# Threshold attention with a feed-forward block: raw weight chunks in the rooms of the turned blocks and exponentials, and chunk work at other places of slots six to ten

## The chip, the cores and the metric

The kernel runs on one core of one Trainium2 chip. The metric is the device time of one execution in microseconds (us); lower is better. Times that are compared are medians of several executions; a profile is one execution, with its own time.

## The reference, cut to what matters

```python
# q, k, v: (8 batches, 8 heads, 576, 64) float32; tau = 0.02
scores = 1/8 * q @ k^T
scores = where(scores >= rowmax(scores) - tau, scores, -1e9)
attn   = exp(scores - rowmax) ; attn /= rowsum(attn) + 1e-9
x      = (attn @ v) with the heads side by side        # (8, 576, 512)
xn     = (x - mean) / sqrt(var + 1e-6) * g_ln
out    = x + relu(xn @ w_ch1) @ w_ch2                  # 512 -> 2048 -> 512
```

Both weight matrices arrive as **float64**. The kernel has to turn them into float32 itself, from the two 32-bit words of each number.

## The kernel before, in words

**Slots.** The attention is cut into 72 slots (`NS`, 9 for each batch), one pass of the loop `for n in range(NS)` (L1072) each. Attention slots are numbered from 0. In a slot, TensorE (PE) makes the scores of four 128 x 576 blocks (L400), VectorE (DVE) takes their maxima (L414), GpSimd (POOL) makes thresholds (L418), ScalarE (ACT) the exponentials (L427), DVE masks and sums them (L434, reciprocals L439), and POOL divides (L450). The exponentials lie in one of two rooms `e_room`: they alternate up to slot 6, and from slot 7 on only `e_room[0]` is used. From slot 6 (`FIRST`) on the blocks are then turned: DVE transposes them in 32 x 32 pieces into `et` (L524, `turn_blocks`), SyncE's queue (SP) sends `et` to a DRAM scratch `scr` (L531, L535) and, in the next slot, fetches `em` and `er` from there (L545 to L554, `fetch`), and PE multiplies them with the values (L593 in the next slot, L603 ahead of the scores of the slot after). Below, turn(7), scr(7), em(7) are those of slot 7. Before slot 6 PE turns the blocks itself (`tp`, `tr`).

**Feed-forward.** A group `g` is half a batch: 288 tokens. `first_part` computes relu(xn @ w_ch1) for 16 column blocks d (PE tile `p`, relu on ACT L791), `second_plain` (only for g = 0) the second product, four blocks m of 16 matmul steps each, whose results ACT copies (L829) and DVE and POOL finish (L705, L706, L711, `add_to_x`, `store`); later groups use `second_quarters`. These steps are drawn in by `second_part(n, i)` (L997) at four places i = 0 to 3 of a slot, so many as a planner's count `owed` says. The PE order of attention and feed-forward is thus fixed when the program is made. All these products share two PSUM banks (tag `ff`): a product waits until ACT has read out the one before the last.

**Weight chunks.** The float64 weights come in 32 chunks of 512 KB (`Weights`): 0 to 15 make up w_ch1, 16 to 31 w_ch2. Each goes through five steps:

- `fetch` (L245): a DMA on SP's queue into a free piece of some room (`piece` takes, of the free pieces that may hold this chunk, the one whose time ends first). Rooms: parts of `w2_sb` that are not written yet, of `hidden`, of an `x` and a `y` tile, and of `stage`. In the profile the rooms have the names `w`, `hidden`, `x_room`, `y_room`, `stage` and `e`.
- `prepare_to` (L267): ACT takes the absolute value of the upper words (L273, "abs") and, at this or a later call, scales the lower words (L278, "low").
- `begin` (L282): three DVE instructions, L288, L291, L295.
- `carry` (L300): a POOL addition (L303), for w_ch1 also a multiplication by g_ln (L306). It gives the piece back, so that a later fetch can use it.
- `begin_to` and `carry_all` run several of these. The table `BEGUN` (L1052) says for each slot up to which chunk `begin` has gone at three places of the slot: `masks_at` (between the maxima and the masks), `behind_at` (behind the masks), `end_at` (at the end of the slot).

`first_part` and `second_plain` don't issue a step whose chunk has not been carried in the order of the program (L779, L820), and on the chip the step waits for that carry's semaphore.

**Order of the queues.** Each engine takes its instructions in the order in which this loop issues them. So a relu that is issued behind three abs waits for them, and SP's next DMA waits until the one ahead of it is issued. `run_all(aside)` issues what `add_to_x`, `store` and `root` (the Newton step on DVE, L732 to L736) left over.

Of the kernel before, what the change touches and what calls it, by code (L numbers as in the profile page):

```python
# [8 lines left out]
F32 = mybir.dt.float32  # L9
# [9 lines left out]
def kernel(  # L19
# [40 lines left out]
    NB = S // 32  # L60
    TOK = S // 2
    QH = 256
    SLOTS = 2 * HP + 1
# [7 lines left out]
    att = ctx.enter_context(tc.tile_pool(name="att", bufs=2))  # L71
# [19 lines left out]
    e_room = [consts.tile([128, 4, S], F32, name=f"e{i}") for i in range(2)]  # L91
# [4 lines left out]
    def product(out, lhsT, rhs, **flags):  # L96


        for h in range(2):
            r = slice(64 * h, 64 * h + 64)  # L100
            nc.tensor.matmul(out[r], lhsT=lhsT[:, r], rhs=rhs, **flags)  # L101
# [75 lines left out]
    class Weights:  # L177
# [13 lines left out]
        def __init__(self):  # L191
            self.chunks = [
                (w1_sb[i][:, c : c + WC], w_ch1[i * 128 : (i + 1) * 128, c : c + WC], i)
                for c in range(0, DF, WC)
                for i in range(NK)
            ] + [
                (
                    w2_sb[:, m, d : d + 4].rearrange("p d c -> p (d c)"),
                    w_ch2[d * 128 : (d + 4) * 128, m * 128 : (m + 1) * 128].rearrange(
                        "(d p) c -> p d c", p=128  # L200
                    ),
                    None,
                )
                for m in range(NK)
                for d in range(0, ND, 4)
            ]
            self.n1 = NK * (DF // WC)
            self.fetched = self.prepared = self.converted = self.begun = self.carried = 0
            self.raw, self.ticks = {}, 2
            flat = lambda t: t.rearrange("p a b -> p (a b)")  # L210

            x_room = ffn.tile([128, NK, TOK], F32, tag="x", bufs=3, name="x_room")
            y_room = ffn.tile([128, NK, TOK], F32, tag="sq", bufs=1, name="y_room")
            stage = self.stage = consts.tile([128, 8, WC], F32, name="stage")

            n1 = self.n1
            self.free = []  # L220
            for t, n, before in (
                (w2_sb.rearrange("p m d c -> p (m d) c"), ND // 2, lambda p: n1 + 2 * p - 6),
                (hidden, 4, lambda p: 10),
                (x_room, 1, lambda p: 2 * n1),
                (y_room, 1, lambda p: 2 * n1),
                (stage, 4, lambda p: 2 * n1),
            ):
                for p in range(n):
                    self.free.append((before(p), -1, flat(t)[:, p * 2 * WC : (p + 1) * 2 * WC]))
# [94 lines left out]
    FIRST = HP + 2  # L324

    def by_blocks(n):

        return n >= FIRST
# [346 lines left out]
    aside, stores, drops = [], [], []  # L675
# [22 lines left out]
    def run_all(calls):  # L698
        now = calls[:]
        calls.clear()  # L700
        for fn in now:
            fn()
# [294 lines left out]
    def second_part(n, i):  # L997

        nonlocal issued, owed, part, now
        part, now = i, QUARTERS * n + i  # L1000
        if not queue:
            return
        at = QUARTERS * n + i
        g = sum(issued >= e for e in ends)
        left = sum(ROOM[t % QUARTERS] for t in range(at, ready(g + 1))) if g + 1 < NG else 0
        owed += (ends[g] - issued) * ROOM[i] / left if left > 0 else 8


        steps = 0
        got = 1 if i in (0, QUARTERS - 1) else 2  # L1010
        while queue and (owed >= 0.5 or got == 1 and i in (0, QUARTERS - 1)):
            got, cost = next(queue[0], (None, 0))
            if got is None:
                queue.pop(0)
                got = 1
            elif got == 0:
                owed = 0.0
                break
            else:
                issued += cost  # L1020
                owed -= cost
                steps += 1
                if steps == 4 and among:
                    mean_of(among[0])
                    centre(among.pop())
# [11 lines left out]
    conversion = Weights()  # L1037
    if w_ch1.dtype == I64:
        conversion.fetch(2)
    else:  # L1040
# [10 lines left out]

    BEGUN = [  # L1052
        (0, 0, 1), (2, 2, 3), (4, 4, 5), (6, 6, 7), (8, 8, 9), (10, 10, 11),
        (13, 16, 17), (19, 22, 22), (25, 27, 27), (29, 31, 31), (32, 32, 32),
    ]

    def constants(times):

        warm = ps_ff.tile([128, QH], F32, tag="ff", name="warm")
        for _ in range(times):  # L1060
            product(warm[:, :128], lhsT=avg_sb, rhs=ident, start=True, stop=True)

    def convert(to):
        conversion.begin_to(to)
        conversion.carry_all()
# [6 lines left out]
    for n in range(NS):  # L1072
        b, s = divmod(n, SLOTS)
        masks_at, behind_at, end_at = BEGUN[min(n, len(BEGUN) - 1)]
        run(n, -3)
        if 0 < n <= HP:
            constants(8 if n > 1 else 26)
        scores(b, s)
        run(n, -2)
        run(n, -1)  # L1080
        if n == FIRST + 1:
            conversion.take(e_room[1])
        if n + 1 < HP:
            scale_q(n + 1, loaded[n + 1][0])
        rest = exponentials(n)
        es, thr = next(rest)
        run(n, 0)
        if n == HP + 2:
            next(rest, None)
        if n >= HP:  # L1090
            conversion.fetch(3, -1 if n > FIRST else 1)
        run_first(stores)
        if n == FIRST:
            convert(masks_at)
        elif n > FIRST + 1:
            conversion.prepare_to(masks_at, False)
        second_part(n, 0)
        while drops and drops[0][0] is nc.gpsimd:
            drops.pop(0)[-1]()
        next(rest, None)  # L1100

        u = (n + 1) // SLOTS * HP + (n + 1) % SLOTS
        if (n + 1) % SLOTS < HP and u < len(units):
            turn(u)
            if u + 1 < len(units) and u != 2:
                load_qk(u + 1 if u > 1 else 3)
        if n < HP:
            conversion.fetch(2 if n else 1)
        if n < SLOTS + HP:
            run_all(aside)  # L1110
        if n != FIRST:
            convert(masks_at)
        conversion.prepare_to(*((end_at,) if n < FIRST else (behind_at, False)))
        run(n, 1)
        second_part(n, 1)
        blocks_go = by_blocks(n)
        diags = weights(es, thr, blocks_go)
        run_all(aside)
        drip()
        if n < SLOTS:  # L1120
            run_all(stores)
        conversion.begin_to(behind_at)
        run(n, 2)
        second_part(n, 2)
        if n < FIRST:
            conversion.carry_all()
        box = []
        if blocks_go:
            conversion.fetch(3, wait=0)
            scr = turn_blocks(b, s, es)  # L1130
            conversion.carry_all()
            at_quarter(n + 1, 0, lambda b=b, s=s, scr=scr, box=box: box.append(fetch(b, s, scr)))
        else:

            made = turn_weights(s, es, diags)
            for i, at in enumerate(
                (-1, -1, 0, 0)
            ):
                if i == 3 and n + 1 == FIRST:
                    at_quarter(n + 1, 0, conversion.prepare_to, BEGUN[n + 1][0], False)  # L1140
                if i < 3:
                    at_quarter(n + 1, at, next, made)
                else:
                    at_quarter(n + 1, at, lambda made=made, box=box: box.append(next(made)))
        at_quarter(
            n + 1, 1 if b == 0 and s <= HP else 3,
            lambda b=b, s=s, box=box: values_of(b, s, box[0]),
        )
        if s in (HP, 2 * HP):
            group_ready(2 * b + (s > HP))  # L1150
        run_all(aside)
        drip({nc.vector: 4, nc.gpsimd: 6})
        if HP <= n < FIRST:
            conversion.fetch(3)
        run(n, 3)
        if b == 0 and s < HP - 1:
            load_v(s + 1)
        elif n >= SLOTS - 2 and (n + 2) % SLOTS < HP and n < NS - 2:
            load_v((n + 2) // SLOTS * HP + (n + 2) % SLOTS)
        if n <= FIRST:  # L1160
            conversion.prepare_to(BEGUN[n + 1][0] - (n == FIRST - 1), n < FIRST)
        second_part(n, 3)
        conversion.begin_to(end_at)
        conversion.carry_all()
        run_all(aside)
        drip({nc.vector: 2, nc.gpsimd: 0})
    while later_calls or queue or aside or stores or drops:
        n += 1
# [38 lines left out]
```

## Time and profile before

| what | value |
|---|---|
| median of 3 runs | 1350.99 us (1350.66 to 1351.26) |
| the profiled execution's own time | 1349.67 us |
| its span, first to last instruction | 1347.7 us (1.97 us lie around it) |
| mean granted TensorE clock | 0.997 |
| PE busy in 80 to 100, 100 to 120, 120 to 140 us | 19.75, 18.15, 17.69 of 20 us |
| PE busy in 140 to 160, 160 to 180 us | 15.71, 17.46 of 20 us |
| PE busy in 180 to 1260 us | 1075.35 of 1080 us |

The scores of slots 6, 7, 8, 9, 10 and 11 start at 70.8, 98.0, 116.4, 137.2, 162.7 and 182.8 us of the span. So the chunks' work, which ends in slot 10, lies in the first 172 us, and the other seven eighths of the span have PE busy throughout. In a timeline line the columns are: start and duration in us, engine (with a q: its queue issues a DMA), line, operation, tiles out<-in, shape, number of instructions merged, and in brackets the idle time before and what ended it.

### The profile page before, as it was taken

How to read it: one execution, taken by the hardware profiler on the slowest of the kernel's cores; microseconds unless marked ns; L12 is line 12 of the kernel's file. 1: busy time of each engine (PE TensorE's matmuls, PEld its weight loads, DVE VectorE, ACT ScalarE, POOL GpSimd, SP SyncE). 2: the span in 40 equal slices, each digit the busy share in tenths (PEclk: the TensorE clock that was granted, in tenths of full speed). 3: DMA queues.
4: the chain of work that ended last, by engine and by line, in shares of the span. 5: the costliest groups of instructions: out<-in, count | busy, mean ns of one | idle time of the engine just before them, and what ended most of it. 6: DMA issues, size and time to landing. Idle time of an engine off the chain costs nothing.

```text
span 1347.7 us, 40452 instructions
## 1 busy us (share of the span) xinstructions
PE 1316.4 (98%) x17400; PEld 995.8 (74%) x17400; DVE 872.4 (65%) x1544; ACT 459.2 (34%) x995; POOL 624.7 (46%) x836
## 2 busy tenths in 40 slices
PE   8998899999999999999999999999999999999997
PEld 7765557769686786968778696877869677786957
DVE  7889876667666675666756677556756667666113
ACT  5866333232423233232233324233232323333120
POOL 3475656535444444444534454443444445335312
PEclk9999899999999999999999999999999999999999
DMA  8918864467643775446644576447754376443211
GB/s 166 304 32 248 205 178 156 158 172 193 178 150 118 197 196 162 151 156 190 178 145 153 162 179 192 141 142 194 198 169 152 123 198 179 134 159 124 81 19 20
DMA packets 335299, 213.94 MB, mean 159 GB/s; under 512 B 247376, under 2 KB 292688, under 8 KB 327056
## 3 DMA queue, kind: packets, MB, share of 16 engines
q1 hardware_dynamic: 329008, 210.46, 54.2%
q8 instruction: 137, 2.24, 0.7%
q10 hardware_dynamic: 5952, 0.74, 0.4%
q0 software_dynamic: 160, 0.15, 0.1%
q14 instruction: 42, 0.34, 0.1%
HBM read 124.00 MB, written 87.29 MB: 157 GB/s over the span
## 4 chain that ended last, share of the span: by engine, by line
PE 91%; DVE 3%; ACT 3%; SPq 1%; DMA 1%; issue 1%; POOL 1%; ACTq 0%; POOLq 0%; DVEq 0%
PE p L101 37%; PE seg L101 30%; PE sc L400 10%; PE sc L593 9%; PE sc L603 2%; ACT e L427 1%; PE tp L101 1%; DVE e L434 1%; SPq L118 1%; PE var L101 1%; DVE neg L414 1%; PE mean L101 0%; ACT em L484 0%; PE pv L593 0%; PE warm L101 0%
## 5 line engine op out<-in xcount | busy, mean ns | idle before, releaser
L101 PE MATMUL p<-xc,w 128*64 128x288 f32 x4096 | 517.0, 408 | 5.5 <-ACT part L878 4.9
L101 PEld LDWEIGHTS p<-xc,w 128*64 128x64 f32 x4096 | 287.9, 137 | 212.2 <-issue 14.3
L414 DVE TENSOR_REDUCE neg<-sc 128x2 f32<-128x1152 f32 x144 | 188.7, 1352 | 286.4 <-PE sc L400 286.1
L450 POOL TENSOR_SCALAR e<-e,den 128x576 f32<-128x576 f32 x264 | 207.4, 798 | 130.0 <-DVE den L439 130.0
L101 PE MATMUL seg<-hidden,w 128*64 128x144 f32 x3840 | 247.9, 287 | 0.0
L101 PEld LDWEIGHTS seg<-hidden,w 128*64 128x64 f32 x3840 | 234.9, 137 | 11.5 <-issue 8.6
L434 DVE SCALAR_TENSOR_TENSOR e<-sc,thr,e 128x576 f32<-128x576 f32 x288 | 222.3, 809 | 18.9 <-POOL thr L418 11.7
L418 POOL TENSOR_SCALAR thr<-neg,low_sb 128x2 f32<-128x2 f32 x144 | 39.8, 277 | 383.5 <-DVE neg L414 382.1
L791 ACT ACTIVATE hidden<-p 128x288 f32<-128x288 f32 x256 | 106.5, 417 | 300.8 <-PE p L101 300.8
L427 ACT ACTIVATE e<-sc,neg 128x576 f32<-128x576 f32 x288 | 198.1, 754 | 2.4 <-DVE neg L414 2.4
L524 DVE STREAM_TRANSPOSE et<-e 128x1152 f32<-128x1152 f32 x118 | 161.2, 1373 | 14.3 <-POOL e L450 13.7
L400 PE MATMUL sc<-kT,qT 64*64 64x384 f32 (+3 forms) x2048 | 138.6, 403 | 1.3 <-DVE e L434 1.2
L593 PE MATMUL sc<-em,v_in 128*64 128x128 f32 (+1 forms) x2368 | 131.2, 265 | 2.6 <-DMA em<-scr 2.6
L593 PEld LDWEIGHTS sc<-em,v_in 128*64 128x64 f32 x2368 | 124.2, 138 | 10.9 <-DVE w L288 2.4
L101 PE MATMUL seg<-hidden,stage 128*64 128x144 f32 x1920 | 123.3, 286 | 0.0
L101 PEld LDWEIGHTS seg<-hidden,stage 128*64 128x64 f32 x1920 | 117.6, 137 | 2.9 <-issue 2.9
L616 ACT COPY x<-sc 128x128 f32<-128x128 f32 x120 | 31.8, 266 | 252.9 <-PE sc L400 182.1
L863 POOL TENSOR_TENSOR hidden<-hidden 128x576 f32<-128x576 f32 x60 | 84.7, 1427 | 51.9 <-ACT hidden L791 42.3
L400 PEld LDWEIGHTS sc<-kT,qT 64*64 64x64 f32 x2048 | 75.8, 133 | 41.7 <-issue 21.4
L878 ACT COPY part<-seg 128x288 f32<-128x288 f32 x74 | 29.8, 403 | 190.6 <-PE seg L101 187.1
L863 DVE TENSOR_TENSOR hidden<-hidden 128x576 f32<-128x576 f32 x60 | 51.1, 886 | 51.5 <-PE seg L101 48.5
L799 POOL TENSOR_TENSOR hidden<-hidden 128x288 f32<-128x288 f32 x48 | 39.5, 822 | 47.1 <-ACT hidden L797 44.6
(121 smaller groups left out, 1077.9 us busy)
## 6 DMA issues: line engine op xcount, KB each, us to landing
scr<-et SPq DMA_DIRECT2D x63, 1152.0 KB, 5.0
em<-scr SPq DMA_DIRECT2D x63, 1024.0 KB, 5.7
out_dram<-ot SPq DMA_DIRECT2D x248, 36.0 KB, 3.8
q_in<-in_q_dram SPq DMA_DIRECT2D x120, 72.0 KB, 2.6
er<-scr SPq DMA_DIRECT2D x132, 64.0 KB, 5.1
k_in<-in_k_dram SPq DMA_DIRECT2D x116, 72.0 KB, 2.8
v_in<-in_v_dram SPq DMA_DIRECT2D x28, 256.0 KB, 5.4
w<-in_moe_w_ch_dram SPq DMA_DIRECT2D x11, 512.0 KB, 6.4
```

The costliest lines, as they stand in the source:

```text
L101: nc.tensor.matmul(out[r], lhsT=lhsT[:, r], rhs=rhs, **flags)
L400: nc.tensor.matmul(sc[h][64 * i : 64 * i + 64, at : at + n], lhsT=ql[r] if s == HP else qT[r, half, j * 128 + 64 * i : j * 128 + 64 * i + 64],
L414: nc.vector.tensor_reduce(out=neg[:, i], in_=pairs[h], axis=AXL.X, op=ALU.max, negate=True,)
L418: nc.gpsimd.tensor_scalar(out=thr[:, i], in0=neg[:, i], scalar1=-1.0, scalar2=low_sb, op0=ALU.mult, op1=ALU.add,)
L427: nc.scalar.activation(es[:, i], blocks[i], func=AF.Exp, bias=neg[:, i : i + 1])
L434: nc.vector.scalar_tensor_tensor(out=es[:, i], in0=blocks[i], scalar=thr[:, i : i + 1], in1=es[:, i], op0=ALU.is_ge, op1=ALU.mult, accum_o ...
L450: nc.gpsimd.tensor_scalar(out=es[:, i], in0=es[:, i], scalar1=den[:, i : i + 1], scalar2=1.0, op0=ALU.mult, op1=ALU.mult,)
L524: nc.vector.transpose(et[:, :, 64 * h : 64 * h + 64].rearrange("p n (j c) -> p j n c", j=2), es[:, 2 * h : 2 * h + 2].rearrange("p j (n c) ...
L593: nc.tensor.matmul(dst[64 * h : 64 * h + 64], lhsT=vt[:, h, c, :], rhs=pick(em[:, 2 * j : 2 * j + 2, c], h), start=c == 0 and first, stop= ...
L791: nc.scalar.activation(hidden[:, d], p1, func=AF.Relu)
L799: nc.gpsimd.tensor_tensor(out=sq[:, 0], in0=sq[:, 0], in1=sq[:, c], op=ALU.add)
L863: eng.tensor_tensor(out=out[at], in0=in0[at], in1=in1[at], op=op)
```

## The change

It has four parts.

1. **Rooms.** The tile of the turned blocks, `et`, which is not used before slot 6, holds two raw chunks (below chunk 13). `e_room[1]` is lent for raw chunks right behind turn(6) instead of at the start of slot 7.
2. **Requests.** `fetch(5)` instead of `fetch(3)` at the end of slots 4 and 5; `fetch(2)` behind turn(6), into the room just lent. By the lists of free pieces, chunks 22 and 23 are now requested in slot 5 and 24 and 25 in slot 6 behind scr(6) (before: all four in slot 7); 26 to 28 in slot 7 (before: 25 to 27 with 22 to 24), 29 to 31 in slot 8 behind em(7) and er(7) (before: 28 to 30 there, and 31 ahead of scr(8)).
3. **Counts.** `BEGUN` runs ahead. Begun by slot, at the three places:

| slot | before | after |
|---|---|---|
| 6 | 13, 16, 17 | 13, 16, 19 |
| 7 | 19, 22, 22 | 21, 23, 24 |
| 8 | 25, 27, 27 | 26, 27, 29 |
| 9 | 29, 31, 31 | 31, 32, 32 |
| 10 | 32 | 32 |

4. **Places.** From slot 7 on the abs for the masks' chunks go behind the slot's last relus (end of the slot before) instead of ahead of the relus; those of `behind_at` go behind `second_part(n, 1)`; those of `end_at` (and, behind them, the lows) ahead of turn. In slots 6 to 10 the two late `run_all(aside)` are left out, so that the Newton step of g = 0 goes from the end of slot 7 to behind the maxima of slot 8, and the finishing of its four results (o, ot, store) goes to later places, the first store from slot 9 to slot 10.

```diff
+            et_room = att.tile([128, NB, 128], F32, tag="et", bufs=1, name="et_room")
...
+                (et_room, 2, lambda p: n1 - 3),
...
-        (13, 16, 17), (19, 22, 22), (25, 27, 27), (29, 31, 31), (32, 32, 32),
+        (13, 16, 19), (21, 23, 24), (26, 27, 29), (31, 32, 32), (32, 32, 32),
...
+    def plain_at(n):
+
+        return FIRST <= n <= SLOTS + 1
...
-        if n == FIRST + 1:
-            conversion.take(e_room[1])
...
-        elif n > FIRST + 1:
-            conversion.prepare_to(masks_at, False)
         second_part(n, 0)
...
-        conversion.prepare_to(*((end_at,) if n < FIRST else (behind_at, False)))
+        if n < FIRST:
+            conversion.prepare_to(end_at)
+        elif n == FIRST:
+            conversion.prepare_to(behind_at, False)
         run(n, 1)
         second_part(n, 1)
+        if n > FIRST:
+            conversion.prepare_to(behind_at, False)
...
             conversion.fetch(3, wait=0)
+            conversion.prepare_to(end_at, False)
             scr = turn_blocks(b, s, es)
+            if n == FIRST:
+                conversion.take(e_room[1])
+                conversion.fetch(2)
             conversion.carry_all()
...
-        run_all(aside)
+        if not plain_at(n):
+            run_all(aside)
...
-            conversion.fetch(3)
+            conversion.fetch(5)
...
-        if n <= FIRST:
-            conversion.prepare_to(BEGUN[n + 1][0] - (n == FIRST - 1), n < FIRST)
+        if n < FIRST:
+            conversion.prepare_to(BEGUN[n + 1][0] - (n == FIRST - 1))
         second_part(n, 3)
         conversion.begin_to(end_at)
         conversion.carry_all()
-        run_all(aside)
+        if FIRST <= n < SLOTS:
+            conversion.prepare_to(BEGUN[n + 1][0], False)
+        if not plain_at(n):
+            run_all(aside)
```

The order of PE's own instructions is the same before and after: the planner draws the same feed-forward steps at the same places of slots 6 to 11, since no step was kept back for a chunk in either order.

## The prediction

> **What bounds the kernel now.** I read the page, then busy time by stretch, then PE's timeline where PE is not full.
>
> ```profile
> span 1347.7 us, 40452 instructions
> ...
> PE   8998899999999999999999999999999999999997
> ```
> ```profile
> 140.00:160.00 20.00, 15.71 (x130) 10.07 (x128) 18.28 (x34) 7.71 (x14) 12.60 (x15) 0.86 0.82 198
> 160.00:180.00 20.00, 17.46 (x168) 10.26 (x166) 15.34 (x31) 6.49 (x13) 9.93 (x14) 0.97 0.74 185
> ```
>
> From 180 us on PE is the bound (1075.35 of 1080 us busy up to 1260): time saved before 180 us moves all that follows forward, and nothing can be saved behind it by this change. Before it PE waits in the chunk stage; the last numbers of a row are the granted clock (0.86 there), DMA share and GB/s. PE's timeline names the waits:
>
> ```profile
> 118.45 4.10 PE L101 MATMUL p<-xc,w 128*64 128x288 f32 x32
> 124.86 8.47 PE L101 MATMUL p<-hidden,w 128*64 128x288 f32 x68 [2.31 <-ACT hidden L791]
> 133.12 1.95 PE L593 MATMUL sc<-em,v_in 128*64 128x128 f32 x32
> 134.87 2.14 PE L101 MATMUL p<-hidden,w 128*64 128x288 f32 x16
> ...
> 152.28 1.19 PE L101 MATMUL p<-hidden,w 128*64 128x288 f32 x8 [1.65 <-POOL w L303]
> 153.92 0.44 PE L593 MATMUL sc<-em,v_in 128*64 128x128 f32 x4 [0.45 <-DMA em<-scr]
> 156.56 3.25 PE L593 MATMUL sc<-em,v_in 128*64 128x128 f32 x28 [2.19 <-DMA em<-scr]
> 159.57 2.95 PE L101 MATMUL p<-hidden,w 128*64 128x288 f32 x16
> ...
> 172.86 2.16 PE L101 MATMUL p<-hidden,w 128*64 128x288 f32 x16 [2.54 <-POOL w L303]
> ```
>
> To see: with a wait of 1.85 us at 106.07 (var, behind a relu) these are five places. At 122.55 and 106.07 a relu lies behind three abs on ACT; at 150.64 and 170.32 a product waits for the carry of chunk 27 and 31; in between PV of slot 8 waits for em(8). From 154.4 to 161.2 us the clock is at half: 28 products take 3.25 us where 32 take 1.95, and 16 take 2.95 where they took 2.14: 1.55 + 0.81 = 2.4 us lost. **Ceiling** of the change: 1.85 + 2.31 + 1.65 + 0.45 + 2.19 + 2.54 + 2.4 = 13.4 us.
>
> The chain that ended last runs from 132 to 151 us over SP's queue, whose timeline shows what makes em(8) late:
>
> ```profile
> 128.76 1.64 SPq L257 DMA_DIRECT2D stage<-in_moe_w_ch_dram  x3
> 130.50 7.19 SPq L118 DMA_DIRECT2D q_in<-in_q_dram  x4
> 137.73 2.67 SPq L118 DMA_DIRECT2D k_in<-in_k_dram  x4
> 140.50 0.91 SPq L257 DMA_DIRECT2D e<-in_moe_w_ch_dram  x1
> 141.51 4.20 SPq L531 DMA_DIRECT2D scr<-et  x4
> ```
>
> et(8) is turned at 140.11, but SP reaches scr(8) at 141.51, with three chunks of 512 KB and q and k ahead of it; four issues of q take 7.19 us, so the DMA engines are full. By the trace's landings k ends at 142.72, chunk 31 at 145.31, scr(8) at 149.68, em(8) at 156.42.
>
> **What the Trainium skill says.** (1) TensorE: Matmul & The Clock Gate, Part 1: the clock halves after an idle window of 3.4 us and returns after a busy one; windows run free. The trace agrees: one stretch at half clock, 6.83 us long, behind the waits around 150 to 156 us; the 2.54 us wait alone brought none. (2) The same page, Architectural detail: ACT and DVE queues are strictly first in, first out; the relus behind the abs agree. (3) SBUF — State Buffer, SBUF: two separate sides: DVE with two SBUF inputs or in a 2-port mode and POOL lock each other out. The trace agrees: begin's three instructions take 0.41, 0.43, 0.69 us at 102.7, and 0.82, 0.80, 1.66 us at 95.2, while POOL carries. (4) DMA: Bandwidth & Descriptors, Issuing engines are not separate DMA queues: all DMAs run on the same 16 engines, so a chunk ahead of scr costs it time; here k, chunk 31 and scr(8) do land one after the other (142.72, 145.31, then up to 149.68).
>
> **The change, part by part.**
>
> *Up to 92.6 us* only rooms and requests differ: chunks 17, 18, 22, 23 are asked for earlier on SP, in 50 to 65 us. Behind them SP has nothing until scr(6) at 95.3: nothing gained or lost.
>
> *Tail of slot 6* (95 to 103 us). Two begins and two carries more ahead of slot 7's maxima and thresholds. DVE before: begin 16 from 95.22 to 98.57, scores at 100.1, maxima at once. After: three begins, between 1.5 us each alone (end 99.9, no loss) and 3.35 each as that one (105.3). I take 2.4, as begins beside POOL's division take: 102.5. Maxima end at 103.9 and 105.2 (1.35 each; before 101.50 and 102.76). POOL: abs 16 to 18 now go ahead of low 13 to 15 on ACT, 3 x 0.58 = 1.75 us, so carry 15 starts at 96.2, not 94.44; three w_ch1 carries take 6.75 as before, to 102.95, three w_ch2 carries 3 x 1.29: 106.8; thresholds 107.4 (before 103.22).
>
> *PE in slot 7.* Two exponentials (1.38) from 103.9, relu of d = 8 to 105.7. PE ends d = 9 at 104.05 and needs that bank: waits 1.7, ends d = 10 at 107.8. Exponentials to 107.0, low 19 and 20 to 108.2, relu to 108.5, var; abs 21 and 22 still stand ahead of the next relu, to 110.1. The product behind var starts at 110.2, before at 108.45: **1.75 lost**, although the change put abs behind one relu.
>
> *turn(7).* Masks wait for thresholds and begins 19, 20: from 108.8 (before 105.72), 3.35 us. Carries 20, 19 to 111.5, division 3.95: 115.45; two begins under it instead of three, to 116.2; turn(7) ends at 118.9 (before 117.48): **+1.4**, from 0 (begins uncontended; POOL's 107.4 then decides) to 6.5 (all begins 3.35).
>
> *Slot 8.* Begin 23 (1.55) takes the place of the Newton step (2.43) ahead of the maxima: they start at 120.5 (before 119.82). No abs ahead of the relus: relu d = 14 at 124.0, PE ends d = 15 at 124.2 and starts `second_plain` at 124.3 (before 124.86): the 2.31 us are gone, 0.5 of it is left after slot 7's loss. em(7) lands 1.4 later, at 133.3: PE, there at 132.5, waits 0.8. So PE's own gain is spent here; it costs nothing, since the next wait swallows it.
>
> *SP in slots 6 and 7.* Chunks 24 and 25 now stand between scr(6) and em(6): 1.1 us of issue and about 3 us of DMA (chunks land 1.5 us apart). em(6) landed at 107.55, er(6) at 108.83; PV of slot 6 comes at 112.8, after at 114.3: hidden, with 2 us left. Fetch 26 waits for carry 18 (104), 27 and 28 for carries 20 and 19 (111.5); behind them stands scr(7), due only at 118.9: free.
>
> *em(8).* SP's slot 8 has the same three chunks at the same place and all of it 1.4 later; chunk 31 is gone from between k and scr(8): 145.31 - 142.72 = 2.6 us of DMA. em(8): 156.42 + 1.4 - 2.6 = 155.2 (bounds: +1.4 if the chunk's share was hidden anyway, -2.6 if turn(7) is on time). The gate of chunk 27 goes, as it is carried at the end of slot 8, but PE then stands at PV by 152 and waits to 155.2 instead: of 4.29 us of waits 3.2 stay. PV starts **1.25 earlier**. Clock: one idle stretch of 3.2 us instead of three pieces; I take the same 2.4 us lost (bounds: none, or 1.7 more for a further half window at half clock).
>
> *Slot 10.* Chunk 31 is carried in slot 9: **2.54 gained**. What is late next: the centring of g = 1 on DVE; maxima 2.6, turn 2.3, two leftovers 0.9 behind scores that end at 164.1 put it at 170.2 to 171.8, when PE is there too (171.8): I take 0.3 off. em(9) is fetched earlier, with the store of m = 0 gone from between; PV of slot 10 has 7 us of room. The stores moved to slots 10 to 12 lie under a full PE: nothing.
>
> **Sum:** -1.25 - 2.54 + 0.3 = -3.5 us: 1349.67 - 3.5 = 1346.2 us of this execution, which is 1.32 us below the median; against the median 1350.99 - 3.5 = **1347.5**.
>
> **Rivals.**
> - *All covers go.* If begins hide (turn(7) on time) and the DMA engines catch up by 4 us, PE doesn't wait for em(8), and the clock stays: 4.29 + 2.4 + 2.54 = 9.2: 1341.8. For it: in slot 7 three chunks are requested instead of six. Against: q, k and three chunks stay ahead of scr(8). Chance 0.15.
> - *Gain given back.* PV no earlier, the longer idle stretch costs another half window (1.7): -2.54 + 1.7 = -0.8: 1350.2. Chance 0.15.
> - *Slower.* Six carries ahead of slot 7's thresholds and three begins ahead of its maxima: one mechanism, on POOL and DVE, that goes through turn(7), scr(7), em(7) and SP to em(8). From turn(7) later by 2.6 + 2.54 = 5.1 us it ends slower. At 6.5, with the further half window: 6.5 - 2.6 - 2.54 + 1.7 = +3.1: 1354.1. For: DVE is 95% busy there. Against: only one begin before took 3.35. Chance 0.2.
> - *It doesn't do what it says* (a chunk is requested earlier but its carry still gates): the counts put carries 27 and 31 a slot's quarter or more ahead; below 0.05, within the second rival.
>
> **Numbers.** Forecast 0.5. What can be told from no change is about 0.2%, 2.7 us: faster means below 1348.3. Of the forecast's 0.5, 0.38 lie below that; with the first rival 0.53. Within: 0.12, the second rival 0.15, 0.05 of the third: 0.32. Slower: 0.15. The range, 1342 to 1353, leaves half of the first rival and most of the third out.
>
> **What would show it.** No wait ahead of `p<-hidden,w` near 123, 151 and 171 us; PE waits in slot 7 of 2.5 us or more ahead of d = 10, var and the next product; maxima of slot 7 at 102 to 103; turn(7) ended at 118 to 120; one wait of PV for em(8) of about 3 us, ended near 155; still one stretch at half clock. Wrong if turn(7) is past 122.6, or if em(8) lands by 152.

## The result and the profile after

| | before | after |
|---|---|---|
| median of 12 executions each | 1350.49 us | 1350.38 us |
| ratio of the times, with its 95% interval | | 1.0003 (0.9996 to 1.0011) |
| the profiled execution's own time | 1349.67 us | 1351.38 us |

The change makes no difference that can be measured. (The ratio is not that of the two medians; the means are 1350.19 and 1350.77 us.) The profiled execution of after lies 1.0 us above its median, that of before 0.8 us below: the two profiles differ by 1.7 us where the medians agree. So single times below are compared by what they stand for, not to the last microsecond.

The page of after, span and the busy shares of PE:

```profile
span 1349.6 us, 40456 instructions
...
PE   8998899999999999999999999999999999999997
```

Busy time by stretch of after: the stretch, its length, busy us of PE (instructions), PE's weight loads, DVE, ACT and POOL, then granted clock, DMA share and GB/s:

```profile
140.00:160.00 20.00, 15.33 (x148) 8.67 (x144) 17.20 (x34) 6.55 (x12) 12.25 (x14) 0.97 0.78 169
160.00:180.00 20.00, 18.95 (x168) 12.03 (x170) 12.58 (x26) 4.27 (x9) 6.49 (x10) 0.85 0.80 195
180.00:1260.00 1080.00, 1075.64 (x14338) 813.74 (x14336) 703.95 (x1224) 341.03 (x753) 501.06 (x686) 1.00 0.56 166
```

Behind 180 us nothing has changed (1075.64 us busy; 1075.35 before). The two stages in front of it are as incomplete as they were: the loss has moved by some microseconds, the low clock with it from the first row to the second. PE's timeline of after says where:

```profile
106.85 3.23 PE L101 MATMUL p<-xc,w 128*64 128x288 f32 x16 [2.64 <-ACT hidden L793]
...
126.44 8.47 PE L101 MATMUL p<-hidden,w 128*64 128x288 f32 x68 [1.26 <-POOL q_in L335]
...
136.61 1.75 PE L595 MATMUL sc<-em,v_in 128*64 128x128 f32 x28 [1.24 <-DMA em<-scr]
...
158.20 0.44 PE L595 MATMUL sc<-em,v_in 128*64 128x128 f32 x4 [3.30 <-DMA em<-scr]
160.50 3.25 PE L595 MATMUL sc<-em,v_in 128*64 128x128 f32 x28 [1.87 <-DMA em<-scr]
163.51 3.27 PE L101 MATMUL p<-hidden,w 128*64 128x288 f32 x16
...
177.07 4.59 PE L101 MATMUL p<-xc,w 128*64 128x288 f32 x36 [0.54 <-ACT o L831]
```

The waits of a product for the carries of chunks 27 and 31 (below, the gates) are gone; 0.54 us for ACT's copy of `o` is new. In their place PV of slot 8 stands before em(8) for 3.30 + 1.87 us (before 0.45 + 2.19). All waits together are 10.85 us, before 10.99. (The releaser in brackets is inferred. At 126.44 it is POOL, but ACT's relu ended at 126.34, 0.1 us ahead of the product: that wait is for the relu, and so is the one put down to POOL `sum` in kernels below.) By the trace's landings:

| us of the span | before | after | difference |
|---|---|---|---|
| turn(6) ended | 95.29 | 95.36 | 0.1 |
| maxima of slot 7 start | 100.14 | 103.57 | 3.4 |
| turn(7) ended | 117.48 | 120.83 | 3.4 |
| SP reaches scr(8) | 141.51 | 145.20 | 3.7 |
| em(8) landed | 156.42 | 160.37 | 4.0 |
| scores of slot 10 start | 162.71 | 166.98 | 4.3 |
| scores of slot 11 start | 182.78 | 185.05 | 2.3 |

The delay arises in the 8 us between turn(6) and the maxima of slot 7, and ahead of its masks, and is handed on. Slot 10 gives 2.0 us back, and that is the removed gate less the new 0.54.

How it arises, from the timeline of DVE and POOL in after at the end of slot 6:

```profile
96.17 0.69 DVE L297 SCALAR_TENSOR_TENSOR w<-w 128x512 uint32<-128x512 uint32 x1
96.28 1.74 POOL L305 TENSOR_TENSOR w<-w,w 128x512 int32<-128x512 int32 x1 [1.91 <-ACT w L280]
96.78 1.53 DVE L290 TENSOR_SCALAR w<-w 128x512 f32<-128x512 f32 x1
...
99.19 1.67 DVE L297 SCALAR_TENSOR_TENSOR w<-w 128x512 uint32<-128x512 uint32 x1
...
101.99 1.67 DVE L297 SCALAR_TENSOR_TENSOR w<-x_room,w 128x512 uint32<-128x512 uint32 x1
...
103.57 2.61 DVE L416 TENSOR_REDUCE neg<-sc 128x2 f32<-128x1152 f32 x2
...
105.42 2.72 POOL L305 TENSOR_TENSOR w<-w 128x512 int32<-128x512 int32 x2
...
108.14 1.40 POOL L420 TENSOR_SCALAR thr<-neg,low_sb 128x2 f32<-128x2 f32 x2
...
110.59 0.81 DVE L436 SCALAR_TENSOR_TENSOR e<-sc,thr,e 128x576 f32<-128x576 f32 x1
```

Begin 16 is done at 96.86 and has hardly a carry beside it. Begin 17 takes 1.53 + 0.81 + 1.67 = 4.0 us beside the carries, begin 18 2.8 us. This fits the lock of the shared pair of ports that the Trainium skill describes (SBUF — State Buffer, SBUF: two separate sides), and it shows on both sides: a carry's addition takes 1.74 us here and 1.29 alone. The scores lay ready from 100.2 on, the maxima start at 103.57, and the masks 4.87 us later than before; with one begin less between masks and turn, 3.35 us of that reach turn(7).

And how it is handed on, SP's queue in after:

```profile
128.56 2.18 SPq L547 DMA_DIRECT2D em<-scr  x4
130.78 1.27 SPq L556 DMA_DIRECT2D er<-scr  x2
132.14 3.07 SPq L259 DMA_DIRECT2D stage<-in_moe_w_ch_dram  x3
135.31 6.13 SPq L118 DMA_DIRECT2D q_in<-in_q_dram  x4
141.49 3.62 SPq L118 DMA_DIRECT2D k_in<-in_k_dram  x4
145.20 4.07 SPq L533 DMA_DIRECT2D scr<-et  x4
149.32 1.60 SPq L133 DMA_DIRECT2D v_in<-in_v_dram  x1
150.97 2.07 SPq L142 DMA_DIRECT2D v_rest<-in_v_dram  x2
153.14 2.18 SPq L547 DMA_DIRECT2D em<-scr  x4
```

From em(7) on SP issues without a pause. turn(8) ended at 139.51, 0.6 us *earlier* than before, and its scr(8) still goes out only at 145.20: what counts is when SP gets there, and that follows em(7), and so turn(7). Chunk 31 is gone from between k and scr(8), which can be seen, and scr(8) is later all the same.

### The profile page after: what moved, and what is told of

The parts are those of the page before. It is cut to its first block, busy times and chain, and to the rows that moved or that the text cites. A ratio compares the mean times of both kernels' runs of the same rounds, so it can differ in the third digit from the quotient of the medians.

```text
span 1349.6 us, 40456 instructions
## 1 busy us (share of the span) xinstructions
PE 1317.8 (98%) x17400; PEld 994.4 (74%) x17400; DVE 873.8 (65%) x1544; ACT 458.9 (34%) x995; POOL 624.9 (46%) x836
## 4 chain that ended last, share of the span: by engine, by line
PE 91%; DVE 3%; ACT 2%; DMA 2%; SPq 1%; issue 0%; POOL 0%; ACTq 0%; POOLq 0%; DVEq 0%
PE p L101 36%; PE seg L101 31%; PE sc L402 10%; PE sc L595 9%; PE sc L605 2%; PE tp L101 1%; ACT e L429 1%; DMA em<-scr 1%; DVE w L297 1%; SPq L533 1%; PE mean L101 1%; PE var L101 1%; ACT em L486 0%; DVE e L436 0%; PE pv L595 0%
## 5 line engine op out<-in xcount | busy, mean ns | idle before, releaser
L101 PE MATMUL seg<-hidden,e 128*64 128x144 f32 x896 | 61.2, 286 | 0.0
```

## The experiments

The theory, formed on this profile: **the counts of slot 6** (begins 17 and 18 and their carries ahead of slot 7's maxima and thresholds) make turn(7) late, SP's queue hands that to em(8), and em(8) takes back what relus and gates gain. Its rivals: the transfer of the chunks, in whatever order, makes em(8) late; the Newton step's new place costs it; or the places in the queues do. Times are medians of five rounds against the kernel before; the line numbers of kernels made from after lie two higher than those of before.

**The counts of slot 6 undone.** After with chunks 17 and 18 begun where they were before.

```diff
-        (13, 16, 19), (21, 23, 24), (26, 27, 29), (31, 32, 32), (32, 32, 32),
+        (13, 16, 17), (19, 22, 24), (26, 27, 29), (30, 32, 32), (32, 32, 32),
```

> The changed kernel with the counts of slot 6 back at 17 begun at its end (16, not 16 to 18), those of slot 7 at 19, 22, 24 and slot 9 at 30, 32, 32; rooms, places and the counts of slot 8 as changed. Chunks 30 and 31 then are requested ahead of scr(8) instead of with 29. Theory (two begins and carries more ahead of slot 7's maxima and thresholds make turn(7) late, and SP's queue hands that on to em(8)): turn(7) ends near 118 us instead of 120.8, em(8) lands near 157 instead of 160.4, the waits for carries stay gone, time some 3 us below both kernels, 1347.4. Rival (the requests hold up em(8), whose queue now has five chunks ahead of scr(8)): em(8) no earlier than 160, time 1350 or more. Rival (what is lost is PE's own wait and half clock in slot 7): time falls by 2 to 3 too, but with em(8) at 160 still ending PE's wait in slot 9.

Measured: 1347.34 us, ratio 0.9977 (0.9970 to 0.9984); turn(7) ended at 117.60, em(8) landed at 157.13. DVE's timeline of this kernel, to be held against that of after:

```profile
100.04 2.62 DVE L416 TENSOR_REDUCE neg<-sc 128x2 f32<-128x1152 f32 x2 [0.98 <-PE sc L402]
...
105.24 0.69 DVE L297 SCALAR_TENSOR_TENSOR w<-x_room,w 128x512 uint32<-128x512 uint32 x1
105.85 0.81 DVE L436 SCALAR_TENSOR_TENSOR e<-sc,thr,e 128x576 f32<-128x576 f32 x1
...
114.97 2.63 DVE L526 STREAM_TRANSPOSE et<-e 128x1152 f32<-128x1152 f32 x2
```

Now the maxima wait for the scores (0.98 us) and the masks start at 105.85 instead of 110.59. turn(7) and em(8) are each 3.2 us earlier than in after and the time is 3 us less, although five chunks instead of three now go out ahead of scr(8): more requests alone don't make em(8) late. PE's timeline of this kernel:

```profile
126.23 10.15 PE L101 MATMUL p<-hidden,w 128*64 128x288 f32 x68 [4.08 <-POOL sum L647]
...
157.26 2.70 PE L595 MATMUL sc<-em,v_in 128*64 128x128 f32 x28 [2.38 <-DMA em<-scr]
```

The wait ahead of the second product is 4.08 us here and 1.26 in after (two begins, 4.6 us beside carries, stand between turn(7) and the maxima of slot 8), and the kernel is still the faster one: what PE loses at 126 us doesn't count, em(8) does. The theory stands, with one thing mixed in: the low clock. Of the two stretches at half clock up to 180 us the one at PV of slot 8 is 3.4 us long here and 6.8 in after. Over all executions the mean granted clock differs little, 0.9964 here and 0.9959 in after.

**The counts of slot 6 alone**, in the kernel before.

```diff
-        (13, 16, 17), (19, 22, 22), ...
+        (13, 16, 19), (19, 22, 22), ...
```

> The kernel before with one edit: 19 instead of 17 in the counts of slot 6, so chunks 17 and 18 are begun and carried at the end of slot 6. No gain of the change is in it. Theory: turn(7) ends near 120.5 us instead of 117.5, em(8) lands near 159.5 instead of 156.4, time 3 us above before, 1353.5. Rival (requests and rooms set em(8)): they are as before, so em(8) near 156.4 and time 1350.5.

Measured: 1351.70 us, ratio 1.0012 (1.0006 to 1.0018): slower, by less than expected. turn(7) ended at 119.51, em(8) landed at 157.90. Against turn(6), which ended 0.7 us later in this profile, turn(7) is 1.3 us late, not 3.4: the chunks 17 and 18 are begun early here, but 19 and 20 then don't stand ahead of the masks of slot 7. So the counts of slot 6 alone make 1.3 of the 3.4 us. That the rest comes with begins 19 and 20 ahead of the masks of slot 7, (21, ..) there, is likely but not shown: no run had those alone.

**The chunks of slot 8 behind scr(8).** After, with chunks 29 to 31 requested right behind scr(8) instead of ahead of q and k.

```diff
+        if n >= HP and n != 8:
             conversion.fetch(3, -1 if n > FIRST else 1)
...
+            if n != 8:
+                conversion.fetch(3, wait=0)
...
+            if n == 8:
+                conversion.fetch(3, wait=0)
```

(Counts of slot 9: 29, 29, 32.)

> The changed kernel, but chunks 29 to 31 are requested right behind scr(8) instead of behind em(7), and begun and carried at the end of slot 9 (counts of slot 9: 29, 29, 32). Theory (em(8) is late because SP's queue comes late to scr(8), behind chunks, q and k): SP reaches scr(8) 3 to 5 us earlier, em(8) lands at 155 to 157 although turn(7) is as late as in the changed kernel, PE's wait in slot 9 shrinks by as much, time 1346 to 1348. Rival (DVE and POOL of slot 8, turn(8), set em(8)): em(8) at 159 or later, time 1350.

Measured: 1351.92 us, ratio 1.0012 (1.0005 to 1.0018). scr(8) is issued at 140.38, right behind turn(8) (140.35) and 4.8 us earlier than in after, and em(8) lands at 159.99, 0.4 us earlier than in after. SP's queue in this kernel:

```profile
133.35 3.10 SPq L118 DMA_DIRECT2D q_in<-in_q_dram  x4
...
140.38 3.81 SPq L533 DMA_DIRECT2D scr<-et  x4
144.29 3.61 SPq L259 DMA_DIRECT2D stage<-in_moe_w_ch_dram  x3
147.94 0.51 SPq L133 DMA_DIRECT2D v_in<-in_v_dram  x1
148.49 1.63 SPq L142 DMA_DIRECT2D v_rest<-in_v_dram  x2
150.22 4.19 SPq L547 DMA_DIRECT2D em<-scr  x4
```

The three chunks now stand between scr(8) and em(8), with the values 5.9 us; em(8) needs SP twice, and what stands ahead of either issue delays it. And SP is not all: em(8) is issued from 150.22, 2.9 us earlier than in after, and gains only 0.4, since by the trace's landings the three chunks land just ahead of it, up to 154.27. That a better order of chunks and scr(8) brings em(8) in falls; the 155 to 157 us that the theory expected did not come. A gate of 1.63 us for a late carry in slot 10 is new.

**Rooms and requests alone**, in the kernel before.

```diff
+                (et_room, 2, lambda p: n1 - 3),
...
-            conversion.fetch(3)
+            conversion.fetch(5)
```

(And the earlier loan of `e_room[1]` with its two requests, from parts 1 and 2 of the change.)

> The kernel before with the rooms and the requests of the change alone (et room, five instead of three, the loan of the exponentials' room and two requests behind turn(6)); counts and places as before. Theory: turn(7) and em(8) within 0.7 us of before, time within 0.1% of before, 1350.5. Rival (requests between scr(6) and em(6) hold up the attention): a wait of PE for em(6) in slot 7 and time 2 us or more above before.

Measured: 1351.46 us, ratio 1.0009 (1.0003 to 1.0016). turn(7) is on time (117.64), but with the old counts five chunks, 27 to 31, are requested in slot 8 ahead of scr(8), which goes out at 143.3; em(8) lands at 158.93, 2.5 us later than before, where at most 0.7 was expected. Asked for earlier in slots 5 and 6, later in slot 8: pieces come free with the carries, and the carries had not moved.

**Places and requests without the counts.** After with the counts of before.

```diff
-        (13, 16, 19), (21, 23, 24), (26, 27, 29), (31, 32, 32), (32, 32, 32),
+        (13, 16, 17), (19, 22, 22), (25, 27, 27), (29, 31, 31), (32, 32, 32),
```

> The changed kernel with the whole table of counts as before; rooms, requests and places as changed. Theory (counts of slot 6 make turn(7) late, em(8) then takes up what PE gains): turn(7) near 117.5 us, em(8) near 157, PE's wait for a relu in slot 8 under 2.3 us, the waits for the carries of chunks 27 and 31 are back, the first inside the wait for em(8), the second 2.5 us in slot 10; time that of before within 0.1%, 1350.4. Rival (the places alone bring the gain that e1 shows): 1347 to 1348.

Measured: 1353.41 us, ratio 1.0019 (1.0012 to 1.0027). PE's timeline of this kernel:

```profile
122.39 8.47 PE L101 MATMUL p<-hidden,w 128*64 128x288 f32 x68
...
153.20 1.19 PE L101 MATMUL p<-hidden,w 128*64 128x288 f32 x8 [3.01 <-POOL w L305]
...
158.19 3.25 PE L595 MATMUL sc<-em,v_in 128*64 128x128 f32 x28 [2.10 <-DVE w L290]
...
174.73 3.59 PE L101 MATMUL p<-hidden,w 128*64 128x288 f32 x16 [3.38 <-POOL w L305]
```

The second product starts at 122.39 without a wait: the places do what they say for the relus. But em(8) lands at 158.05, and both gates are there, longer than before (1.65 and 2.54). The last wait for em(8) is named DVE in the view; em(8) landed 0.14 us ahead of its end. Neither the theory (1350.4 us) nor the rival (1347 to 1348) had this time: five chunks stand ahead of scr(8) as with rooms and requests alone, and the mean granted clock of its executions is 0.9940 where that of before is 0.9960. Held against the kernel with the slot 6 counts undone (1347.34 us), it says that the counts from the end of slot 7 to slot 9 remove the gates. That those of slot 6 and of the masks of slot 7 cost time is what the kernel with the slot 6 counts undone says.

**The Newton step back in slot 7**, in after; two relus of slot 8 wait for it there, as the lines further below show.

```diff
-        if not plain_at(n):
+        if n == 7 or not plain_at(n):
             run_all(aside)
```

> The changed kernel with one edit: the Newton step of g = 0 back at the end of slot 7 (in the changed kernel it runs in slot 8, and the relus of d = 14 and 15 end their wait with it, since they write the part of hidden that it reads). Theory (em(8) sets when slot 9 goes on): whatever PE gains or loses in slot 8 is taken up by its wait for em(8), time within 0.1% of the changed kernel, 1350.4. Rival (the moved Newton step is what the change lost): PE reaches the second product 1 us earlier and time falls by 1 us or more.

Measured: 1349.72 us, ratio 0.9997 (0.9989 to 1.0005). No difference to after that can be measured. The second product starts at 127.45, later than in after: with late turn(7) the step and begin 23 both stand ahead of the maxima.

**The step back and the counts of slot 6 undone**, with fewer begins in slot 7.

```diff
-        (13, 16, 19), (21, 23, 24), (26, 27, 29), (31, 32, 32), (32, 32, 32),
+        (13, 16, 17), (19, 22, 22), (25, 27, 28), (30, 32, 32), (32, 32, 32),
...
-        if not plain_at(n):
+        if n == 7 or not plain_at(n):
```

> The changed kernel with the counts of slots 6 and 7 as before, those of slots 8 and 9 at 25, 27, 28 and 30, 32, 32, and the Newton step back at the end of slot 7. In e1 PE still waited 4.1 us in slot 8 behind the begins of chunks 22 and 23 and the Newton step; both are out of the way of slot 8's exponentials and relus here. Theory (em(8) sets the time): PE reaches the second product 2.5 us earlier than in e1, em(8) lands at 156 to 157 as there, time within 0.7 us of e1, 1347.3. Rival (PE's own waits count): 1345 or less.

Measured: 1348.48 us, ratio 0.9985 (0.9978 to 0.9991). The second product starts at 124.12, 2.1 us earlier than with the slot 6 counts undone alone, and the time is not lower. em(8) landed at 157.60 (157.13 there): a second sign that gains ahead of em(8) are swallowed. The time of 1345 us or less, expected if PE's own waits count, did not come.

**Three chunks behind em(8).** The same, with chunks 29 to 31 requested only behind em(8).

```diff
-            conversion.fetch(3, -1 if n > FIRST else 1)
+            conversion.fetch(2 if n == 8 else 3, -1 if n > FIRST else 1)
...
+            if n != 8:
+                conversion.fetch(3, wait=0)
```

(Counts of slots 8 and 9: 25, 27, 29 and 29, 29, 32.)

> As e7, but chunks 29 to 31 are requested behind em(8) and er(8) in slot 9 and begun and carried at its end (counts 25, 27, 29 and 29, 29, 32), so two chunks instead of five are requested between em(7) and em(8). Theory (em(8) is set by the whole of what the DMA engines have to move between em(7) and em(8), which e3, with the same amount in another order, left as it was): em(8) lands near 153, time 3 us or more below e7, about 1344. Rival (q, k and turn(8) set em(8), as chunk 31, taken out by the change, brought only 0.3 us): em(8) at 156 or later, time as e7.

Measured: 1351.67 us, ratio 1.0010 (1.0002 to 1.0018). em(8) lands at 154.99, 2.6 us earlier than with those chunks ahead, and a gate brings it back:

```profile
168.60 6.49 PE L101 MATMUL p<-hidden,w 128*64 128x288 f32 x28 [3.58 <-POOL w L305]
```

The 28 products take 6.49 us, where 36 took 4.59 in slot 10 of after: the clock is at half there. With their begins at the end of slot 9, three chunks can't all go behind em(8).

**The values behind em(8).** A different thing ahead of em(8), in which no chunk is touched: the three DMAs of slot 8's `load_v`, put behind em(8) and er(8). Once on the kernel with the slot 6 counts undone, once on before, once on after.

```diff
-            load_v((n + 2) // SLOTS * HP + (n + 2) % SLOTS)
+            if n == 8:
+                at_quarter(n + 1, 0, load_v, (n + 2) // SLOTS * HP + (n + 2) % SLOTS)
+            else:
+                load_v((n + 2) // SLOTS * HP + (n + 2) % SLOTS)
```

> As e1, and the three loads of values that slot 8 requests between scr(8) and em(8) go behind em(8) and er(8); nothing of the chunks is changed. Theory (PE's wait for em(8) sets when slot 9 goes on): em(8) lands 2 to 3 us earlier than in e1, near 154.5, PE's wait of 2.4 us nearly goes, time 2 us below e1, near 1345.3. Rival (another wait takes its place at once): within 0.7 us of e1, 1347.3.

> The kernel before with the loads of values of slot 8 behind em(8) and er(8) as the only edit. Theory: em(8) lands near 153.7 us instead of 156.4; PE still waits for the carry of chunk 27 to 152.3 and then hardly for em(8): PV of slot 8 some 2.7 us earlier, time near 1347.7. Rival (em(8) does not set the time): within 0.7 us of before, 1350.4.

> The changed kernel with the loads of values of slot 8 behind em(8) and er(8) as the only edit. Theory: em(8) lands near 157.5 us instead of 160.4, time 2.5 us below the changed kernel, near 1347.8. Rival (em(8) does not set the time): within 0.7 us of the changed kernel, 1350.4.

| base of the edit | median | ratio to before | em(8) landed, without and with the edit |
|---|---|---|---|
| slot 6 counts undone | 1345.35 us | 0.9961 (0.9948 to 0.9973) | 157.13, 156.05 |
| before | 1348.64 us | 0.9989 (0.9981 to 0.9996) | 156.42, 155.28 |
| after | 1345.95 us | 0.9971 (0.9959 to 0.9983) | 160.37, 157.82 |

The first of them beats both kernels, by 5 us. On after the way up to scr(8) is as it was. SP's queue with the edit:

```profile
145.22 4.10 SPq L533 DMA_DIRECT2D scr<-et  x4
149.43 4.22 SPq L547 DMA_DIRECT2D em<-scr  x4
153.71 1.28 SPq L556 DMA_DIRECT2D er<-scr  x2
```

scr(8) goes out at 145.22 as in after (145.20) and lands at the same time (153.23, 153.16); em(8) is issued from 149.43 instead of 153.14 and lands 2.55 us earlier. Issue and bandwidth both have a part: its last piece goes out 1.53 us earlier (153.29, 154.82) and then lands in 4.53 us instead of 5.55. On the other two bases em(8) gains only 1.1 us, where 2 to 3 were expected: SP is free earlier, but the pieces of em(8) wait there for those of scr(8) to land.

PE's timeline of after with the edit, and of the fastest kernel:

```profile
157.96 1.75 PE L595 MATMUL sc<-em,v_in 128*64 128x128 f32 x28 [1.87 <-DMA em<-scr]
159.50 2.14 PE L101 MATMUL p<-hidden,w 128*64 128x288 f32 x16
```

```profile
126.77 10.83 PE L101 MATMUL p<-hidden,w 128*64 128x288 f32 x68 [4.09 <-POOL sum L647]
...
155.71 2.23 PE L595 MATMUL sc<-em,v_in 128*64 128x128 f32 x32
157.74 2.14 PE L101 MATMUL p<-hidden,w 128*64 128x288 f32 x16
```

In the fastest kernel the wait for em(8) is gone. On after em(8) still ends PE's wait, and the time falls by 4.4 us (5.2 between the two profiles), more than the 2.55 of em(8). In the profiles the rest is clock: in after these 28 and 16 products took 3.25 and 3.27 us, at half clock, and here 1.75 and 2.14, so 2.6 us less. The trace of after with this edit has no stretch at half clock up to 1341 us.

So em(8) was the bound, and what the change gains behind it depends on the counts of slot 6. Without them the rest of the change is worth 3.1 us with the values in their old place (0.9977), and with the values moved on both sides about 3.8 us (0.9961 against 0.9989; 1.8 to 5.7 from both intervals), at the same mean granted clock over all executions (0.9966 and 0.9964). The whole change, with the values moved on both sides, is worth about 2.4 us (0.9971 against 0.9989; 0.5 to 4.3), but there the clock differs, 0.9977 against 0.9964. In the 172 executions of before the time falls by 0.7 us for each 0.001 of granted clock; by that, an estimate, 0.9 of the 2.4 us is clock. What is left is not clear of zero.

**Chunk 31 alone**, in the kernel before: requested behind em(8) instead of ahead of scr(8), the very DMA whose removal the prediction put at 2.6 us.

```diff
+            if n != 8:
                 conversion.fetch(3, wait=0)
```

> The kernel before with one edit: chunk 31 is requested behind em(8) and er(8) in slot 9 instead of ahead of scr(8); it is still begun and carried in slot 10. It measures by itself the term by which the prediction let em(8) gain. As the prediction had it (2.6 us of DMA out of the way): em(8) lands near 153.8 us instead of 156.4, time 2 us or more below before, 1348.4. As the changed kernel and e8 suggest (a chunk ahead of scr(8) costs em(8) well under 1 us, since SP's own issue of q, k and scr takes the time): em(8) at 155.5 to 156.4, time within 0.1% of before.

Measured: 1348.02 us, ratio 0.9984 (0.9976 to 0.9992). SP's queue in this kernel:

```profile
137.57 2.67 SPq L118 DMA_DIRECT2D k_in<-in_k_dram  x4
140.34 4.14 SPq L531 DMA_DIRECT2D scr<-et  x4
```

scr(8) goes out right behind turn(8) (140.21), 1.2 us earlier than before; em(8) lands at 155.55, 0.9 earlier. So the 2.6 us of the prediction did not come; scr(8) could go out at most 1.4 us earlier, since turn(8) stands next. The time falls by 2.2 us (1.1 to 3.2), more than em(8) moved: PE waits once for 1.64 us, and the products behind that wait run at full clock (28 in 1.75 us; 3.25 before), while two stretches of 3.4 us at half clock stand elsewhere.

## Why the prediction was right or wrong

The time lies inside the range, and no change had a chance of 0.32; but the forecast of −3.5 us did not come, and the step on which it rested, em(8), failed. That the range holds the result is owed to its width and its rivals, not to that mechanism. What came is the rival **"gain given back"** (1350.2 us: PV no earlier, the 2.54 us of slot 10 gained and lost), carried by the mechanism of the **slower** rival (carries and begins, turn(7), em(8)), which stopped short of ending slower.

- **Tail of slot 6, mis-sized.** Begins were taken at 2.4 us each; 17 and 18 took 4.0 and 2.8, and 19 and 20 stood between maxima and masks for 4.5 us (106.1 to 110.6) instead of 3.6. The thresholds were done at 109.54, not 107.4. So turn(7) came 3.4 us late instead of **+1.4**. The page of before had one begin beside carries, at 3.35 us; that was the nearest row, and a value from beside the division was taken in its place.
- **PE in slot 7, right in kind.** Waits of 2.5 us or more were predicted; one of 2.64 us came, with products at half clock behind it. The product behind var starts at 110.94 (110.2 predicted).
- **Slot 8, partly.** No abs ahead of the relus is right, and with turn(7) on time and no begin between it and the maxima the wait is gone (old counts: 122.39); with turn(7) on time and two begins there it is 4.08 us (slot 6 counts undone). Missed: the Newton step, moved behind the maxima, reads and writes `hidden`, of which the relus of d = 14 and 15 write a part. In after they wait for it:

```profile
125.38 0.46 DVE L737 TENSOR_TENSOR hidden<-hidden 128x288 f32<-128x288 f32 x1
...
125.93 0.41 ACT L793 ACTIVATE hidden<-p 128x288 f32<-128x288 f32 x1 [0.64 <-DVE hidden L737]
...
126.85 0.41 ACT L793 ACTIVATE hidden<-p 128x288 f32<-128x288 f32 x1 [0.51 <-DVE rb L738]
```

  A new wait, added by the change and not named: 1.15 us here. With the step back in slot 7 it is gone, and the time is the same.
- **em(8), the step that failed.** The sum was +1.4 − 2.6 = −1.2; it came out at +4.0. Of the difference of 5.2 us, 2.0 are turn(7)'s. The other 3.2 are the chunk's −2.6 and a rest of 0.6. The chunk was priced as DMA time (landings of k and of the chunk); what its removal bought by itself, in one pair of profiles, is 0.9 us of em(8) and 1.2 of scr(8)'s issue, about its place in SP's queue (0.91 us). The prediction's own reading, turn(8) at 140.11 and scr(8) at 141.51, allowed 1.4 us at most for the issue. In after SP reaches scr(8) by way of em(7), q and k, with the chunk away, and it is 3.7 us late. The upper bound that the prediction had named, +1.4 "if the chunk's share was hidden anyway", would have been nearer for this term.
- **Slot 10, right.** The gate is gone, something smaller is late next: −2.0 us measured, −2.54 + 0.3 predicted. Only it is not the centring on DVE, it is ACT's copy of `o` (0.54).
- **Clock, nearly.** In the place of PV still one stretch of 6.8 us, as forecast; a second, of 3.4 us, came behind the wait in slot 7 and costs about 1.1 us (16 products in 3.23 us, 2.1 at full clock). The Trainium skill's window of 3.4 us (TensorE: Matmul & The Clock Gate, Part 1) fits the lengths, 3.41 and 6.83. Its *idle* window, which the prediction took over, does not fit: in before PE was busy for 1.63 of the 3.41 us ahead of the stretch (150.99 to 154.40). The changes of clock of a trace lie whole multiples of 3.41 us apart; they fix a grid of windows, and in the 14 traces, from 20 us on and by PE's modelled ends, it shows a threshold instead. All 33 windows at full clock with PE busy below 40% are followed by half clock, none of the 5350 above 48%; of nine between, three are. Half clock ended behind every window with PE busy 92% or more and behind none of 72% or less. So what a wait costs depends on how the fixed windows cut it: the wait of 2.6 us in slot 7 leaves a window of 28% in after, and a stretch follows; with the values moved it leaves 41%, and none does.

So of −1.25 − 2.54 + 0.3 the first term was wrong in sign: PV of slot 8 starts 4 us later, in the profiled pair; if slot 10 gives 2.0 us back in every execution, the loss ahead of it is about as large in the medians, which agree. The rest of 0.6 us in em(8) is no more than single profiles differ by. From turn(7) to scr(8) take 24.4 us in after, 23.4 in after with the values moved and 22.4 with the Newton step back, three kernels with the same DMAs on SP up to there. From turn(7) to em(8), with the values in their old place, it is 37.3 us with two chunks in slot 8, 38.0 to 39.5 with three, 38.4 and 38.9 with four, and 39.2 to 41.3 with five (39.5 with the slot 6 counts undone). **Open** is how much of each gain is clock; no run held the clock fixed, and the estimate above is all there is.

## What to carry to other kernels

Before work is pulled ahead, follow each queue that it enters to the next transfer that leaves behind it: here begins on DVE moved a store, a load behind it, and the wait that ends a slot 60 us on. Time gained on an engine ahead of a wait that another engine ends is swallowed; first undo what makes that wait later (here the counts of slot 6 and of the masks of slot 7), or move it (here three DMAs). And price a DMA that is taken out of an in-order queue by its issue and by its bandwidth apart, look at what stands next (here turn(8), then the landing of scr(8)), and keep the smaller until a run shows the larger: chunk 31 stood for 0.9 us of issue and 2.6 of DMA and was worth 0.9.

## What was not expected of the hardware

- **Issue time.** The four issues of a `scr` store hold SP for 3.8 to 5.7 us, and for 3.83 us even where nothing lies ahead (scr(6) in after, at 95.39): the first two take 0.34 and 0.50 us, the next two 1.22 and 1.65, while from 96.3 to 99.3 us the store's own packets keep the DMA engines 76 to 79% busy. How long q's four issues take does depend on the chunks ahead: 3.10 us with none (chunks behind scr(8)), 4.59 with two, 6.13 and 7.19 with three (after and before). So the prediction's reading of q's issues as full DMA engines holds (the DMA share in before is 1.07 while they go out); whether an issue is long by itself or by its own packets is not shown. The Trainium skill (DMA: Bandwidth & Descriptors, Issuing engines are not separate DMA queues) calls the time to initiate a DMA "usually small relative to the DMA itself". Here it is not small: the values' issues took 3.7 us between scr(8) and em(8), and the values landed within 2.4 us of scr(8).
- **Contention.** Beside POOL's carries and their multiplications a begin took up to 4.0 us, alone 1.5.
- **Spread.** Single executions of before lie between 1346.7 and 1353.9 us, so a pair of profiles can differ by 2 us where the medians don't.
